# Batch 3's keys and queries loaded in three parts, with the first part re-laid out ahead of batch 2's last FFN units

## The chip, the cores and the metric

The kernel runs on one core of a Trainium2 chip. The metric is the device time of one execution in microseconds, as a median of several runs: 398.33 us for the kernel before (three runs, 398.25 to 398.63). A profiled execution is longer than its own span by what lies before the first and behind the last instruction.

Names of engines below: PE is TensorE (matmul), PEld its weight loads, DVE is VectorE, ACT is ScalarE, POOL is GpSimd, SP is SyncE. POOL and SP work here as issuers of DMAs more than as engines; an issued DMA is carried out by 16 DMA engines that the issuers' queues share.

## The reference

Sigmoid attention over 8 batches, 12 heads, 448 positions and a head size of 64, followed by a gated feed-forward network (FFN) over the 3584 rows that the attention gives:

```python
scores = scale * np.matmul(q, k.transpose(0, 1, 3, 2)) - np.log(S)
attn = 1.0 / (1.0 + np.exp(-scores))
x = np.matmul(attn, v)            # heads put side by side: 3584 x 768
gate = np.maximum(x @ w_gate, 0.0)
val = x @ w_val
out = gate * val @ w_out          # 1536 -> 768
```

## The kernel before

**Attention.** The heads of a batch are worked in three groups `g` of four heads. For QK, keys and queries have to stand with the head's 64 elements on the partitions. They come from DRAM the other way round, converted to fp16 on the way (`load`, line 106, issued on POOL's queue). For batch 2 and later they are turned by `dma_transposes(b, g)` (line 211): two DVE copies re-lay a group's keys and queries into a tile `rel` (line 215, 128 x 896 each), and one DMA transpose, issued on SP's queue, turns `rel` into `qkT` (line 219). `rel` has two buffers, `qkT` three. A QK unit (`qk_unit`, line 292) takes one of seven column blocks of a group: 4 matmuls on PE into two PSUM banks, and two sigmoids on ACT. The 21 units of a batch go group by group, seven units each; after a group's seventh unit its product with V (`pv_group`, 28 matmuls) follows a few units later.

**FFN.** Batches 0 and 1 are multiplied with `w_gate` and `w_val` in units `gv` (line 304): 12 matmuls, a ReLU on ACT, a product on DVE into `hT` (line 327). Later batches, and the product with `w_out`, go in pairs with fewer block products (`gv_pair`, `down_pair`), which need sums of blocks made ahead on DVE: `weight_sums(i)` (line 376, 1.35 us each) makes the four sums of `w_out`'s blocks.

**The order.** The schedule is manual: each engine's queue has the order in which the code calls. Batch `b`'s loop (line 692) cuts the 21 QK units into stretches `m` by `cuts`, and behind each stretch come FFN units. For batch 2, `mix` says how many `gv` units follow each stretch, and `hooks[m]` puts other work between them: a hook `(left, work)` runs when `left` units are still to come. `ffn_mix` (line 574) does that:

```python
for left in range(count, -1, -1):
    while hooks and hooks[0][0] >= left:
        hooks.pop(0)[1]()
    if left:
        gv_queue.popleft()()
```

Batch 2's last stretch (`m` = 5) has three QK units, two `gv` units and a `down_pair` (line 758), whose `jobs` run behind its first product. In the kernel before, the hooks of this stretch are `weight_sums(1)` between the two units and `weight_sums(2)` behind them, and the jobs are `dma_transposes(3, 0)` and `dma_transposes(3, 1)` followed by `weight_sums(3)`. `dma_transposes(3, 2)` comes in batch 3's first stretch.

**Loads.** Batch 3's keys, queries and values are loaded in batch 2's first stretch (line 750): one load each for `k` and `q`, and three for `v` (`load_v`). On POOL's queue they stand behind batch 2's values and the two loads of `w_out` (`load_o`), and ahead of `hold(3, 2)` (line 645), a small copy on POOL that waits until a transpose has landed, and batch 4's loads. The tiles `k16` and `q16` have one buffer from batch 2 on, so a load waits until the batch before it has been re-laid out.

Of the kernel before, what the change touches and what calls it, by code (L numbers as in the profile page):

```python
# [17 lines left out]
def kernel(  # L18
# [75 lines left out]
    def tiles_of(b):  # L94
        if b not in in_tiles:
            pool = early if b == 1 else inp
            in_tiles[b] = tuple(
                p.tile([P, NPAIR, NCH * D], FP16, tag=t, name=t)
                for p, t in ((pool, "k16"), (pool, "q16"), (vinp, "v16"))
            )  # L100
        return in_tiles[b]

    def rows_of(src, b):
        return src[b].rearrange("(x r) (t c) d -> (r t) x (c d)", r=2, c=NCH)

    def load(b, g0, g1, which, c0=0, c1=NCH):
        for nm, t16, src in zip("kq", tiles_of(b), (k, q)):
            if nm in which:
                xs, cs = slice(2 * g0, 2 * g1), slice(c0 * D, c1 * D)
                nc.gpsimd.dma_start(t16[:, xs, cs], rows_of(src, b)[:, xs, cs])  # L110

    def load_v(b):
        v16 = tiles_of(b)[2]
        nc.gpsimd.dma_start(v16[:, 0::2, :], rows_of(v, b)[:, 0::2, :])
        for r in range(2):
            nc.gpsimd.dma_start(
                v16[64 - 64 * r : P - 64 * r, 1::2, :], rows_of(v, b)[64 * r : 64 * r + 64, 1::2, :]
            )
# [71 lines left out]
    def qkT_of(b, g):  # L190
        if (b, g) not in qkT_tiles:
            qkT_tiles[(b, g)] = qkTp.tile([P, TW, P], FP16, tag="qkT", name="qkT")
        return qkT_tiles[(b, g)]
# [17 lines left out]
    def dma_transposes(b, g):  # L211
        k16, q16, _ = in_tiles[b]
        rel = relp.tile([P, TW, P], FP16, tag="rel", name="rel")
        for ti, t16 in enumerate((k16, q16)):
            nc.vector.tensor_copy(  # L215
                rel[:, ti * NCH : (ti + 1) * NCH, :].rearrange("p c (h d) -> p h c d", h=2),
                t16[:, 2 * g : 2 * g + 2, :].rearrange("p h (c d) -> p h c d", c=NCH),
            )
        nc.sync.dma_start_transpose(
            qkT_of(b, g)[:], rel[:].rearrange("p c x -> p (c x)")  # L220
        )
# [70 lines left out]
    def qk_unit(b, g, c):  # L292
        ps = [bank("qk_ps") for _ in range(2)]
        qk(qkT_tiles[(b, g)], c, 0, NCH, lambda hh: ps[hh][:, 0:S])
        PT = PTp.tile([P, 2, S], FP16, tag="PT", name="PT")
        for hh in range(2):
            sigmoid(PT[:, hh, 0:S], ps[hh][:, 0:S])
        PT_tiles[(b, g, c)] = PT

    def pv_group(b, g):  # L300
        pv(b, g, 0, S, [PT_tiles.pop((b, g, c))[:, :, 0:S] for c in range(NCH)])
# [66 lines left out]
    def open_late():  # L368
        first_sbuf.close()
        pool = ctx.enter_context(tc.tile_pool(name="late", bufs=1))  # L370
        late["T"] = pool.tile([P, 4, HF, HM], FP16, tag="T", name="T")
        late["X"] = pool.tile([P, 3, HD, S], FP16, tag="X", name="X")
        late["sums"] = ctx.enter_context(tc.tile_pool(name="sums", bufs=2))

    def sub(o, a, b):
        nc.vector.tensor_tensor(out=o, in0=a, in1=b, op=AOP.subtract)
# [18 lines left out]
    def weight_sums(i):  # L395
        T = [late["T"][:, j] for j in range(4)]
        B11, B21 = wo[:, 0:HF, 0:HM], wo[:, HF:NFC, 0:HM]
        B12, B22 = wo[:, 0:HF, HM:DM], wo[:, HF:NFC, HM:DM]
        sub(T[i], *((B12, B11), (B22, T[0]), (B22, B12), (B21, T[1]))[i])
# [96 lines left out]
    def batch_sums_t1(g):  # L496
        T1, _, _, B11, _, B12, _ = batch_blocks(g, (0, HD))
        sub(T1, B12, B11)

    def batch_sums(g, ks):  # L500
        T1, T2, T4, _, B21, B12, B22 = batch_blocks(g, ks)
        sub(B12, B22, B12)
        sub(T2, B22, T1)
        sub(T4, B21, T2)
# [69 lines left out]
    def ffn_mix(count, hooks=()):  # L574
        hooks = list(hooks)
# [5 lines that stand above are left out]
# [56 lines left out]
    def pv_finish(b):  # L637
        pv_group(b, NG - 1)
        if b < 2:
            push_gv(b, 0, S, range(NFC))  # L640
# [4 lines left out]
    def hold(b, g):  # L645
        nc.gpsimd.tensor_copy(gate[0:1, :], qkT_tiles[(b, g)][0:1, 0, 0:2])

    def both(b, g):
        pe_transposes(b, g, 0)
        pe_transposes(b, g, 1)  # L650
# [10 lines left out]
    def push_group(g):  # L661
        tail = [("t", g, 6)] + [("y", g, p) for p in range(3)]
        if g == 0:
            tail.insert(0, tail.pop(1))
        work.extend([("w", g, f) for f in range(0, NFC, 2) if g > 0] + tail)
# [26 lines left out]
    for b in range(1, B):  # L692
        if b == 1:
            cuts, pv_at = (0, 3, 6, 9, 13, 17, 21), {3: (0, 2), 5: (1, 2)}
        elif b == 2:
            cuts, pv_at = (0, 4, 7, 11, 14, 18, 21), {0: (-1, 2), 2: (0, 2), 4: (1, 2)}
        else:
            cuts, pv_at = (0, 4, 8, 12, 16, 21), {0: (-1, 2), 2: (0, 2), 4: (1, 2)}
        count = len(cuts) - 1
        hooks = {}  # L700
        if b == 1:
            mix = (3, 3, 3, 3, 3, 2)
            hooks = {
                1: [(1, lambda: both(1, 1))],
                3: [(1, lambda: both(1, 2))],
                4: [(3, lambda: dma_transposes(2, 0))],
                5: [(2, late_loads)],
            }
        elif b == 2:
            mix = (2, 2, 1, 1, 1, 2)  # L710
            hooks = {
                2: [(0, prepare)],
                4: [(0, lambda: weight_sums(0))],
                5: [(1, lambda: weight_sums(1)), (0, lambda: weight_sums(2))],
            }
            open_late()
        elif b == 3:
            mix = (1, 1, 1, 0, 0)
        else:
            mix = (0,) * count  # L720
        for m in range(count):
            jobs = []
            for i, (g, c) in enumerate(order[cuts[m] : cuts[m + 1]]):
                if m in pv_at and i == pv_at[m][1]:
                    if m == 0:
                        pv_finish(b - 1)
                        if b == 2:
                            push_group(0)
                        elif b % 2 == 0:
                            push_group(b // 2 - 1)  # L730
                    else:
                        pv_group(b, pv_at[m][0])
                qk_unit(b, g, c)
            if m == 0 and b > 1:
                jobs.append(lambda: dma_transposes(b, 2))
            if b == 2 and m == count - 1:
                jobs.append(lambda: (dma_transposes(3, 0), dma_transposes(3, 1)))
            elif b == 3 and m == count - 1:
                jobs.append(lambda: (dma_transposes(4, 0), dma_transposes(4, 1)))
            elif 0 <= m - count + 2 and 3 < b < B - 1:  # L740
                jobs.append(lambda: dma_transposes(b + 1, m - count + 2))
            if b == 1:
                if m == 0:
                    load(2, 0, 1, "kq")
                    load(2, 1, 2, "kq")
                    load(2, 2, 3, "kq")
            elif m == 0 and b + 1 < B:
                if b == 3:
                    jobs.append(lambda: hold(3, 2))
                jobs.append(lambda: (load(b + 1, 0, 3, "kq"), load_v(b + 1)))  # L750
            if b % 2 and b > 2:
                if m == count - 1:
                    jobs.append(lambda: (batch_sums_t1(b // 2), batch_sums(b // 2, (0, 1))))
            elif b > 3 and m == 0:
                jobs.append(lambda: batch_sums(b // 2 - 1, (1, HD)))
            if b == 2 and m == count - 1:
                ffn_mix(mix[m], hooks[m])
                next_work(jobs + [lambda: weight_sums(3)], first_act=True)
            elif mix[m]:
                for job in jobs:  # L760
                    job()
                ffn_mix(mix[m], hooks.get(m, ()))
            else:
                next_work(jobs)
            if b == 3 and m in (1, 3):
                for f in range(*((0, 8, 2), (8, NFC, 2))[m // 2]):
                    gate_sums(f, f + 2)
# [35 lines left out]
```

## Time and profile before

| what | us |
|---|---|
| median of 3 runs | 398.33 |
| the profiled execution | 399.14 |
| its span | 397.3 |
| PE busy | 388.5 |
| DVE, ACT, POOL busy | 279.6, 223.2, 49.5 |
| batch 2's last two gv units on PE | 89.37 to 94.1 |
| its down_pair on PE | 93.9 to 100.9 |
| batch 3's first QK units on PE | from 101.36 |
| batch 3's loads of k, q: issue, time to landing | 74.0, 18.4 and 74.8, 21.0 |
| w_out's second load: issue, time to landing | 73.0, 16.0 |
| transpose of batch 3's group 0: issue, time to landing | 96.75, 4.6 |

Times within the profile count from the first instruction. The busy time of PE is 98% of the span, but the end of a matmul is modelled, so an idle stretch of PE is what tells of a wait. A line of the timeline or of a group gives the engine, the line of the code, the operation, what it writes `<-` what it reads, shapes, and in brackets how long the engine had been idle and what ended that. "SPq" and "POOLq" are the issuing queues of these engines. In the DMA view q0 is the queue of POOL's loads, q1 that of the transposes and stores issued by SP and ACT, and q8 and q14 fetch instructions; its columns are packets, MB and the time that the packets took as a share of 16 engines' time (over 100% where packets overlap).

### The profile page before, as it was taken

What the parts mean: (1) busy time and instruction counts of PE and PEld (TensorE: products, weight loads), DVE (VectorE), ACT (ScalarE), POOL (GpSimd) and SP (SyncE); (2) the same over time, 40 slices, a digit from 0 to 9 for tenths busy, and PEclk for the clock granted to TensorE, in tenths of its full rate; (3) what the DMA queues carried; (4) which work ended last, traced back from release to release, by engine and by line L of the source; (5) the groups of instructions that cost most, each with busy time, mean ns of one, the idle gap of its engine ahead of it and who ended that gap; (6) DMA issues with size and microseconds to landing.
All of it is one profiled execution on the core that took longest, in us unless ns stands there. A gap on an engine that the chain in (4) does not pass through costs nothing.

```text
span 397.3 us, 8744 instructions
## 1 busy us (share of the span) xinstructions
PE 388.5 (98%) x3488; PEld 217.5 (55%) x3488; DVE 279.6 (70%) x539; ACT 223.2 (56%) x476; POOL 49.5 (12%) x73
## 2 busy tenths in 40 slices
PE   8999999999999999999999999999999999999995
PEld 3678686445455554554555555455455555555563
DVE  3453345358377889999758889999776779987662
ACT  5946768684785565655665455565566233543121
POOL 8643400700030300003000300000000000000000
PEclk9999999999999999999999999999999999999999
DMA  9999994999999893224945695222013320000135
GB/s 150 196 198 204 206 129 87 180 203 190 203 143 180 167 218 53 46 48 54 177 84 133 130 219 89 48 21 57 19 40 81 81 79 2 0 1 2 40 94 146
DMA packets 68953, 43.69 MB, mean 110 GB/s; under 512 B 35888, under 2 KB 65584, under 8 KB 68912
## 3 DMA queue, kind: packets, MB, share of 16 engines
q0 software_dynamic: 30736, 23.33, 39.2%
q1 hardware_dynamic: 37744, 19.34, 23.2%
q8 instruction: 27, 0.44, 0.4%
q10 hardware_dynamic: 432, 0.46, 0.4%
q14 instruction: 14, 0.11, 0.1%
HBM read 47.19 MB, written 11.01 MB: 146 GB/s over the span
## 4 chain that ended last, share of the span: by engine, by line
PE 84%; DMA 11%; POOL 2%; ACT 1%; issue 0%; DVE 0%; ACTq 0%; POOLq 0%; DVEq 0%
PE u L385 32%; PE g L385 15%; PE y L385 8%; PE qk_ps L232 7%; PE pv_ps L250 7%; PE g_ps L309 5%; PE v_ps L309 5%; DMA wg<-in_moe_w_gate_dram 4%; DMA v<-in_v_dram 3%; PE ya L346 3%; DMA q<-in_q_dram 2%; PE yb L346 1%; DMA qkT<-rel 1%; ACT PT L187 1%; POOL k L110 1%; POOL q L110 1%
## 5 line engine op out<-in xcount | busy, mean ns | idle before, releaser
L187 ACT ACTIVATE PT<-qk_ps 128x448 f16<-128x448 f32 (+3 forms) x318 | 150.5, 595 | 72.6 <-PE qk_ps L232 72.5
L385 PEld LDWEIGHTS <-S 128*128 128x128 f16 x540 | 52.8, 98 | 43.6
L536 DVE TENSOR_TENSOR gsb<-g,gsb 128x448 f32<-128x448 f32 x72 | 42.9, 625 | 14.6 <-PE g L385 14.1
L232 PE MATMUL qk_ps<-qkT 64*64 64x448 f16 (+2 forms) x756 | 49.9, 336 | 1.3 <-DVE qkT L206 0.5
L421 ACT ACTIVATE ysb<-u 128x384 f32<-128x384 f32 x27 | 13.4, 498 | 53.4 <-PE u L385 53.4
L327 DVE TENSOR_TENSOR hT<-gate_sb,v_ps 128x256 f16<-128x256 f32 (+2 forms) x36 | 16.2, 465 | 34.7 <-ACT gate_sb L318 22.3
L532 ACT COPY gsb<-u 128x448 f32<-128x448 f32 x48 | 25.7, 566 | 23.9 <-PE u L385 22.9
L250 PE MATMUL pv_ps<-PT,v 64*64 64x448 f16 (+2 forms) x756 | 37.7, 329 | 1.1 <-DMA v<-in_v_dram 0.8
L184 DVE TENSOR_SCALAR xT<-pv_ps 128x448 f16<-128x448 f32 (+2 forms) x53 | 27.9, 567 | 15.2 <-PE pv_ps L250 13.8
L385 PEld LDWEIGHTS <-hT 128*128 128x128 f16 x288 | 27.7, 98 | 19.8 <-issue 2.1
L232 PEld LDWEIGHTS <-qkT 64*64 64x64 f16 x756 | 20.0, 105 | 25.5 <-issue 16.3
L309 PE MATMUL v_ps<-xT,wv 128*128 128x256 f16 (+2 forms) x216 | 33.3, 290 | 0.3 <-DMA wv<-in_moe_w_val_dram 0.3
L309 PE MATMUL g_ps<-xT,wg 128*128 128x256 f16 (+2 forms) x216 | 33.5, 291 | 0.1
L385 PEld LDWEIGHTS <-wv 128*128 128x128 f16 x216 | 21.1, 98 | 19.7
L385 PEld LDWEIGHTS <-wg 128*128 128x128 f16 x216 | 20.3, 98 | 20.6 <-issue 3.0
L250 PEld LDWEIGHTS <-v 64*64 64x64 f16 x756 | 21.8, 107 | 12.8 <-DMA v<-in_v_dram 1.5
L385 PE MATMUL u<-T,hT 128*128 128x384 f16 x144 | 27.3, 326 | 0.0
L437 DVE SCALAR_TENSOR_TENSOR ysb<-y,ysb 128x384 f32<-128x384 f32 x24 | 13.4, 557 | 17.8 <-PE y L385 10.3
L309 PEld LDWEIGHTS <-wg 128*128 128x128 f16 x216 | 18.5, 98 | 11.5 <-issue 5.0
L110 POOL DMA_DIRECT2D k<-in_k_dram x14 | 10.9, 780 | 110.7 <-DVE rel L215 104.4
L309 PEld LDWEIGHTS <-wv 128*128 128x128 f16 x216 | 20.1, 98 | 7.9 <-DMA wv<-in_moe_w_val_dram 0.6
L385 PE MATMUL u<-xT,wg 128*128 128x448 f16 x108 | 23.5, 353 | 0.1
(69 smaller groups left out, 531.0 us busy)
## 6 DMA issues: line engine op xcount, KB each, us to landing
out_dram<-ysb SPq DMA_DIRECT2D x52, 192.0 KB, 3.0
k<-in_k_dram POOLq DMA_DIRECT2D x5, 672.0 KB, 11.7
q<-in_q_dram POOLq DMA_DIRECT2D x5, 672.0 KB, 14.9
v<-in_v_dram POOLq DMA_DIRECT2D x8, 336.0 KB, 15.4
v<-in_v_dram POOLq DMA_DIRECT2D x16, 168.0 KB, 15.2
k<-in_k_dram POOLq DMA_DIRECT2D x8, 224.0 KB, 10.4
wo<-in_moe_w_out_dram POOLq DMA_DIRECT2D x1, 1536.0 KB, 13.1
q<-in_q_dram POOLq DMA_DIRECT2D x6, 224.0 KB, 11.3
```

What stands on the lines that cost most here:

```text
L110: nc.gpsimd.dma_start(t16[:, xs, cs], rows_of(src, b)[:, xs, cs])
L184: nc.vector.tensor_scalar(out=xT, in0=src, scalar1=XSCALE, scalar2=None, op0=AOP.mult)
L187: nc.scalar.activation(PT_ap, ps_ap, AF.Sigmoid, bias=sig_bias, scale=qk_scale)
L232: nc.tensor.matmul(out_of(hh)[o : o + 64, :], qkT[rows, c, cols], qkT[rows, NCH + c0 : NCH + c1, cols], start=True, stop=True, tile_positi ...
L250: nc.tensor.matmul(ps[hh][64 * r : 64 * r + 64, 0:qn], v16[rows, 2 * g + hh, c * D : (c + 1) * D], pieces[c][rows, hh, :], start=(c == 0), ...
L309: nc.tensor.matmul(ps[-1][:, 0:qn], wt[:, dc, f * P : (f + 1) * P], xT_tiles[b][:, dc, q0 : q0 + qn], start=(dc == 0), stop=(dc == NDC - 1),)
L327: nc.vector.tensor_tensor(out=hT_tiles[g][:, f, o : o + qn], in0=gate_sb[:, 0:qn], in1=ps[1][:, 0:qn], op=AOP.mult,)
L346: nc.tensor.matmul(ps[:, 0 : m1 - m0], hT_tiles[g][:, f, t * P : (t + 1) * P], wo[:, f, m0:m1], start=(f == 0), stop=(f == NFC - 1),)
L385: nc.tensor.matmul(ps[:, 0:n], A[:, k_, :], W[:, k_, :], start=(first and k_ == 0), stop=(k_ == kn - 1), skip_group_check=True,)
L421: nc.scalar.activation(o, ps[:, 0:HM], AF.Copy, scale=OUT_SCALE)
L532: by(gs[u][i][:], ps[u][:, 0:S])
L536: nc.vector.tensor_tensor(out=gs[u][i][:], in0=ps[u][:, 0:S], in1=gs[u][i][:], op=AOP.add)
```

## The change

Batch 3's keys and queries are loaded group by group, six loads instead of two, in the order k and q of group 0, of group 1, of group 2; the bytes are the same. `dma_transposes(3, 0)`, that is two DVE copies and the DMA transpose, is moved from the jobs of batch 2's last `down_pair` to a hook ahead of the two last `gv` units. `dma_transposes(3, 1)` stays where it is. Other batches' loads and transposes are not changed.

```diff
                 4: [(0, lambda: weight_sums(0))],
-                5: [(1, lambda: weight_sums(1)), (0, lambda: weight_sums(2))],
+                5: [
+                    (2, lambda: dma_transposes(3, 0)),
+                    (1, lambda: weight_sums(1)),
+                    (0, lambda: weight_sums(2)),
+                ],
...
             if b == 2 and m == count - 1:
-                jobs.append(lambda: (dma_transposes(3, 0), dma_transposes(3, 1)))
+                jobs.append(lambda: dma_transposes(3, 1))
...
-                jobs.append(lambda: (load(b + 1, 0, 3, "kq"), load_v(b + 1)))
+                def load_next():
+                    for g0, g1 in ((0, 1), (1, 2), (2, 3)) if b == 2 else ((0, 3),):
+                        load(b + 1, g0, g1, "kq")
+                    load_v(b + 1)
+
+                jobs.append(load_next)
```

## The prediction

> **What bounds the kernel now.** I read the page first: TensorE (PE) is busy for 388.5 of 397.3 us, so only an idle stretch of PE can be won or made. The busy table by windows says where those are.
>
> ```profile
> 100.90:101.40 0.50, 0.06 (x5) 0.05 (x8) 0.00 (x0) 0.45 (x1) 0.00 (x0) 1.00 1.28 224
> 101.40:393.00 291.60, 291.12 (x2218) 155.12 (x2218) 232.48 (x438) 153.74 (x334) 14.84 (x21) 1.00 0.46 87
> ```
>
> The columns are stretch, length, then busy us (and instructions) of PE, weight loads, DVE, ACT, POOL, then clock, DMA share, GB/s. From 101.4 us on PE lacks 0.48 us in 291.6, so whatever delays it at 101.4 is paid at the end nearly in full, and whatever is won there is kept. The chain of waits from 85 to 105 us shows what ends the idle stretch.
>
> ```profile
> 96.03 0.72 PE u L385 x5
> 96.75 4.56 DMA qkT<-rel
> 101.31 0.04 issue
> 101.36 0.57 PE qk_ps L232 x8
> ```
>
> Batch 3's first QK units wait for the transpose of its group 0, which was issued at 96.75 us and landed at 101.31. PE's work before that ends at 100.91 (the list of waits puts 0.4 us on it, the idle time before 101.36 in the timeline is 0.45). So the place that the change touches holds **0.45 us, 0.11% of the time**: no gain can be larger, and it is under the 0.2% that a measurement of this kernel can tell from no change (0.80 us). A loss has no such ceiling.
>
> The timeline shows DVE around the new place of the re-layout.
>
> ```profile
> 89.39 1.35 DVE L376 TENSOR_TENSOR T<-wo 128x2304 f16<-128x2304 f16 x1
> 92.36 0.62 DVE L327 TENSOR_TENSOR hT<-gate_sb,v_ps 128x448 f16<-128x448 f32 x1 [1.62 <-ACT gate_sb L318]
> 96.75 4.87 SPq L219 DMA_TRANSPOSE qkT<-rel  x2
> ```
>
> Last, the DMA view. Loads (q0) and transposes (q1) share the 16 DMA engines. Three windows: loads alone (89 to 92 us), both together (138 to 141), a transpose alone (106 to 108.5).
>
> ```profile
> q0 software_dynamic: 701, 0.61, 126.4%
> ...
> q0 software_dynamic: 514, 0.45, 91.1%
> q1 hardware_dynamic: 516, 0.13, 33.2%
> ...
> q1 hardware_dynamic: 1789, 0.46, 98.5%
> ```
>
> The first number is packets. Loads alone pass 701 in 3 us, 234 a us. A transpose alone passes its 1,789 packets in 2.3 us (the DMA row of that window is empty until 106.25), 780 a us. Together they take turns one for one, 514 to 516 in 3 us: **a transpose beside loads runs at 172 packets a us, under a quarter of its pace**.
>
> **The change part by part.**
>
> *Three loads for each of k and q.* POOL issues six loads instead of two. An issue of a third takes 0.71 us (batch 2's, at 40 to 49 us), of a whole 0.84: 6 x 0.71 - 2 x 0.84 = 2.6 us more on POOL, which idles from 77.6 to its hold at 109.3 waiting for a transpose. So this costs nothing itself. Behind these on POOL's queue stand V's three loads. In the built program POOL's loads take eight completion semaphores in turn, and with four loads more V's parts come onto those of the two wo loads and of k's first third, and wait for them. By the DMA issues wo's second part was issued at 73.0 and landed 16.0 later, at 89.0; the first landed at 85.1. So V is issued at about 85, 89 and 90 us, still ahead of its turn (q lands at 74.8 + 21.0 = 95.8), and the load queue doesn't run dry. PE needs V only at batch 3's first PV group, at 110 us. Nothing on the path. Packets per byte stay the same.
>
> *When the first third is there.* After wo (89.0), k landed at 74.0 + 18.4 = 92.4 and q at 95.8, so 3.4 us for each, 1.13 for a third: k's group 0 at 90.1, q's at 91.3.
>
> *The re-layout moved.* Two DVE copies of 0.39 us go from behind weight sum 2 (96.0 us) to behind weight sum 0, which ends at 89.39 + 1.35 = 90.74. The k copy runs at once, the q copy waits until 91.3 and ends at 91.7. DVE had nothing to do until 92.36, so it costs nothing there; the cover is 0.66 us. If q's third came later than 92.0, the hT product at 92.36 behind it, and the banks that it frees, would be late. At its old place it takes 0.6 us away before weight sum 3, which PE's last product needs only at 99.8: no gain.
>
> *The transpose moved.* SP issues it when the copies are done (0.07 us later at the old place), at 91.8 instead of 96.75. SP has nothing between: group 1's transpose and the stores from 101.7 on keep their order behind it. Its first packets come 1.15 us after the issue (105.11 to 106.25), at 92.95. This is what the change is about, and here it meets the loads, as the DMA view of 92.9 to 99 us shows:
>
> ```profile
> q0 software_dynamic: 1178, 1.00, 102.4%
> q1 hardware_dynamic: 487, 0.12, 20.8%
> q8 instruction: 1, 0.02, 0.9%
> q14 instruction: 1, 0.01, 0.3%
> ```
>
> 1,178 load packets are still to come. Taking turns, they and 1,178 of the transpose's 1,790 need 1,178 / 172 = 6.85 us, to 99.8. The other 612 at 780 a us need 0.8, to 100.6. From last packet to landing 109.2 - 108.5 = 0.7 us: **101.3 us, to a tenth the landing of before**. Five microseconds of earlier issue are given to the loads: before, the transpose came to engines that had just run out of them.
>
> *The instruction fetch.* The last two lines above are fetches, at 93 and 96 us. Where a fetch falls into a transpose beside loads, all engines stand still for a while. The transpose issued at 183.9 had one; this is the GB/s row of 184 to 195 us, 0.275 us a figure:
>
> ```profile
> GB/s 0 0 0 2 95 153 164 163 145 142 140 116 133 146 154 170 168 162 175 172 170 181 191 192 197 202 191 187 194 242 182 187 183 101 50 25 9 121 191 207
> ```
>
> The fall to 101, 50, 25, 9 is about 1.2 us. The three transposes issued together with loads landed 10.6 us (225.3, no fetch), 11.5 (183.9, a fetch) and 12.2 us after issue (133.8, a fetch): 0.9 and 1.6 more. Before, the fetch at 96 us fell ahead of the transpose's packets, though a shorter hole of some 0.75 us shows at 98.5. Now it falls in the middle. I add 1.1 us: landing at 102.4. The ends: without a hole 101.3 (and 0.4 less if the count is generous, 100.9); with the full 12.2 us of the worst row, 91.8 + 12.2 = 104.0. I stand near 91.8 + 10.6 = 102.4, the row without a fetch but with more loads beside it than here; two ways to the same figure.
>
> *What follows.* PE's wait is then 102.4 + 0.05 - 100.9 = 1.55 us instead of 0.45, **+1.1 us**. Group 1's transpose queues behind it: 102 + 2.3 + 0.7 = 105.0, needed by batch 3's eighth unit at about 107 + 1.1. V, pushed back by some 3.5 us from 99.4, is needed at 110 + 1.1. The hold and batch 4's loads shift with PE. Sum: 399.14 (profiled execution: span 397.3 and 1.84 around it) + 1.1 = 400.2; that execution stands 0.81 above the median, so the prediction is 398.33 + 1.1 = **399.4 us**.
>
> *A rule weighed.* The row first: the load queue's 126.4% share from 89 to 92 us says that the engines have no spare time where the transpose now goes. The Trainium skill (Perfetto Trace Analysis, DMA Optimizations) says that splitting DMAs can let some of the work start sooner, and expects a sooner end if the DMA engines are generally idle. Taken without its condition it gives a landing at 91.8 + 4.1 = 95.9, PE's wait gone and 398.7 us for the profiled execution; by the rows it is 400.2, since the condition doesn't hold here.
>
> **The rivals.**
>
> *Likeliest, 0.60: late by a hole or by more sharing*, landing 102.0 to 103.4, 399.0 to 400.4 us.
>
> *A draw, 0.22*: landing 101.0 to 101.7, between -0.3 and +0.4 us, 398.0 to 398.7. For it: the count of packets without a fetch. Against: a fetch falls in the window, and fetches cost both transposes that had one beside loads.
>
> *It does what it says, 0.10*: the transpose lands before 100.9, PE doesn't wait, 398.33 - 0.45 = 397.9. This is the other side. The place is the same wait of PE at 101.36; it decides if the transpose needs no more than 9.1 us from its issue at 91.8. For it: 4.1 us with free engines, and the loads end before it does. Against: 10.6 to 12.2 us in all three cases with loads.
>
> *Worse, 0.08*: 12.2 us, or a first third that lands after 92 us and holds DVE, landing at 104 or later: +2.7, 401.0.
>
> **How the numbers follow.** 80%: 398.1 leaves out most of the third case, 400.7 most of the last and the edge of the first. The likeliest's own range is 399.0 to 400.4. Slower by over 0.2% (399.13): most of the likeliest and the last, 0.62. Faster by over 0.2% (397.53) needs 0.8 us where 0.45 are to be had: 0.03 for what I haven't seen. The rest, 0.35, within.
>
> **What the profile after would show.** Right: the transpose issued at about 91.8 and landing at 102 or later; PE idle for over 1 us before batch 3's first qk_ps, ended by that DMA; q0 and q1 with equal packet counts from 94 to 99 us; V landing at about 103 instead of 99.4; DVE's hT still at 92.4. Wrong: the transpose landing in under 9 us although the loads run (no taking turns), or rel's q copy far from 91.5 (thirds land otherwise), or a wait elsewhere, such as V in batch 3's first PV group.

## The result, and the profile after

The changed kernel takes 399.16 us (median of 11 runs, 398.90 to 400.33) against 398.33 of the kernel before: a ratio of 1.0022 with a 95% interval of 1.0014 to 1.0030, 0.83 us slower. The prediction was 399.4.

Where it is lost, two views of the changed kernel's profile show. The chain of waits from 85 to 110 us (start, length, what):

```profile
90.09 0.96 PE v_ps L309 x6
91.06 10.47 DMA qkT<-rel
101.52 0.04 issue
101.57 0.57 PE qk_ps L232 x8
```

The transpose of batch 3's group 0 is issued 5.7 us earlier than before (91.06 against 96.75) and lands 0.2 us later (101.52 against 101.31): it takes 10.47 us where it took 4.56. Lines of the timeline around it:

```profile
90.60 0.39 DVE L215 COPY rel<-q 128x896 f16<-128x896 f16 x1
91.06 10.06 SPq L219 DMA_TRANSPOSE qkT<-rel  x2
91.77 0.62 DVE L327 TENSOR_TENSOR hT<-gate_sb,v_ps 128x448 f16<-128x448 f32 x1 [0.78 <-ACT gate_sb L318]
101.57 0.57 PE L232 MATMUL qk_ps<-qkT 64*64 64x448 f16 x8 [1.25 <-DMA qkT<-rel]
```

PE's idle time ahead of batch 3 has grown from 0.45 to 1.25 us. These 0.80 us agree with the 0.83 us of the medians. Behind it nothing has changed, as the busy table by windows says (PE had 291.12 busy of these 291.60 us before):

```profile
101.40:393.00 291.60, 291.09 (x2218) 155.15 (x2218) 232.53 (x438) 153.74 (x333) 14.88 (x21) 1.00 0.46 87
```

The spans of the two profiles (397.3 and 397.5 us) differ by only 0.2: in the profile after, PE's work ahead of the wait ends at 101.57 - 1.25 = 100.32 us, 0.59 earlier than before. That comes from ahead of the change: a transpose at 63 us is already 0.75 earlier (issued at 62.97 against 63.72), and the first load that the change touches is issued at 73 us. In the profile before PE waited 0.78 us for V's load at 48 us, in that after it did not. Times within profiles are therefore to be read against the end of PE's work in the same profile.

### The profile page after: what moved, and what is told of

Same layout as the page of the kernel before. It is cut to its first block, busy times and chain, and to the rows that moved or that the text cites. A ratio compares the mean times of both kernels' runs of the same rounds, so it can differ in the third digit from the quotient of the medians.

```text
span 397.5 us, 8750 instructions
## 1 busy us (share of the span) xinstructions
PE 388.7 (98%) x3488; PEld 218.0 (55%) x3488; DVE 279.9 (70%) x539; ACT 223.3 (56%) x476; POOL 52.2 (13%) x77
## 4 chain that ended last, share of the span: by engine, by line
PE 93%; ACT 3%; DMA 3%; DVE 1%; issue 0%; ACTq 0%; DVEq 0%
PE u L385 32%; PE g L385 15%; PE qk_ps L232 9%; PE y L385 8%; PE pv_ps L250 8%; PE g_ps L309 7%; PE v_ps L309 7%; PE ya L346 3%; DMA qkT<-rel 3%; ACT PT L187 2%; PE warm_ps L175 1%; PE yb L346 1%; PE trt L201 1%; DVE qkT L206 0%; ACT ysb L421 0%
## 5 line engine op out<-in xcount | busy, mean ns | idle before, releaser
L110 POOL DMA_DIRECT2D k<-in_k_dram x16 | 12.3, 768 | 111.1 <-DVE rel L215 104.5
```

## The experiments

The theory, A: what the moved transpose gains by its early issue it loses again to the loads that run beside it, and a fetch that falls into it adds to that. The rivals: the split loads or the late V cost the time (C); the issue on SP is what is slow (B); DVE's new order costs it. The table has all runs of the study, with the landing of group 0's transpose and PE's idle time ahead of batch 3 (from each kernel's profile), and the ratio of times to the kernel before on the same chip. The kernel before ran again beside each set of runs; its median was 398.42 us beside split alone, move alone and the two kernels with all of V behind, and 398.33 beside the rest. The diffs are cut to the lines that matter and are against the changed kernel, except for "before, V behind" and "before, fetch moved", which are against the kernel before.

| kernel | issue, us to landing | PE idle ahead of batch 3 | median us | ratio, 95% interval |
|---|---|---|---|---|
| before | 96.75, 4.6 | 0.45 | 398.33 | 1 |
| changed | 91.06, 10.5 | 1.25 | 399.16 | 1.0022 (1.0014 to 1.0030) |
| split alone | 96.53, 4.7 | 0.58 | 398.26 | 0.9998 (0.9989 to 1.0006) |
| move alone | 94.97, 4.9 | 0, but 2.4 ahead of it | 400.73 | 1.0059 (1.0043 to 1.0074) |
| changed, V behind | 91.17, 7.3 | 0 | 398.25 | 0.9992 (0.9983 to 1.0001) |
| changed, half of V behind | 90.78, 9.0 | 0 | 398.07 | 0.9993 (0.9983 to 1.0002) |
| before, V behind | 95.60, 4.1 | 0, but 1.4 later | 399.85 | 1.0032 (1.0021 to 1.0042) |
| changed, one unit later | 92.57, 7.6 | 0.34 | 398.11 | 0.9992 (0.9983 to 1.0001) |
| changed, fetch moved | 91.56, 9.7 | 0.82 | 399.00 | 1.0014 (1.0005 to 1.0023) |
| before, fetch moved | 96.41, 4.3 | 0.16 | 398.61 | 1.0006 (0.9997 to 1.0015) |

### The split alone

```diff
-                    (2, lambda: dma_transposes(3, 0)),
...
-                jobs.append(lambda: dma_transposes(3, 1))
+                jobs.append(lambda: (dma_transposes(3, 0), dma_transposes(3, 1)))
```

> The loads in three parts alone, the transpose of group 0 at its old place. If the loss comes from the moved transpose (theory A), six loads instead of two and the later issue of V cost nothing: the time of before, 398.3 us to 0.3 us, PE's wait ahead of batch 3 0.45 us as before. If the split itself costs (rival: the later V, or thirds that move fewer bytes a microsecond), most of the 0.8 us is here: 398.9 to 399.2 us.

398.26 us, a ratio of 0.9998. PE's wait is close to that of before, in this kernel's timeline:

```profile
101.27 0.38 PE L232 MATMUL qk_ps<-qkT 64*64 64x448 f16 x4 [0.58 <-DMA qkT<-rel]
```

The six loads and the later issue of V cost nothing that can be measured. C falls.

### The move alone

```diff
-                    for g0, g1 in ((0, 1), (1, 2), (2, 3)) if b == 2 else ((0, 3),):
+                    for g0, g1 in ((0, 3),):
```

> The re-layout and transpose moved, with whole loads. Group 0's q copy then waits for the whole of q (95.8 us in the profile before), DVE stands from 90.7 to there, and weight sums 1 to 3 behind it come late: sum 1 ends at 95.8 + 0.4 + 0.6 + 1.35 = 98.2 instead of 94.25, and PE's second product with it, at 95.9 before, waits 2.3 to 2.7 us. Both theories: about 2.3 us above before, 400.6 us (400.0 to 401.3), with the idle time of PE inside the down_pair and the transpose no longer what PE waits for. If the old place was harmless for DVE, it stays at 399.2.

400.73 us, where 400.6 was expected. The list of waits from 88 to 104 us (engine and line, what it waited for, us in total, times, longest):

```profile
DVE rel L215 <- DMA q<-in_q_dram: 3.0, 1, 3.0
PE u L385 <- DVE T L376: 1.9, 1, 1.9
```

DVE waits for the whole of q, and PE for the weight sum queued behind it. So the split is what makes the new place possible at all. PE's wait for the transpose is gone here, and it helps nothing: a later one has taken its place.

### V behind the transpose

```diff
-                    (2, lambda: dma_transposes(3, 0)),
+                    (2, lambda: (dma_transposes(3, 0), hold(3, 0), load_v(3))),
...
-                    load_v(b + 1)
+                    if b != 2:
+                        load_v(b + 1)
```

> The changed kernel, but batch 3's V is loaded only after the transpose of group 0 has landed (a second small POOL copy that waits for it). Theory A (the transpose is late because loads share the DMA engines with it): the loads beside it end with q, at about 95 us; 520 packets taking turns at 172 a us from 92.2 are through at 95.2, the other 1,270 at 780 a us at 96.9, landing at 97.6, with a hole of 1.2 us 98.8. PE no longer waits: 398.33 - 0.45 = 397.9 us. Theory B (what is slow is the issue on SP, 3.9 us to the first packet in the changed kernel, whatever is queued): first packet at 95, landing at 97.8, 397.9 us too; the time to the first packet tells them apart (1.2 us by A, 3.9 by B). If V's load has no part in it, 399.2 us.

The transpose lands at 98.45, and PE goes from the `down_pair` into batch 3's QK units without a gap; the chain of waits has no DMA in it:

```profile
99.39 0.97 PE u L385 x6
100.36 0.50 PE qk_ps L232 x8
```

398.25 us: 0.91 below the changed kernel, and 0.9992 of before, where 0.9989 was expected; the interval reaches to 1.0001, so that it beats the kernel before isn't shown. That V's load, which in this stretch does nothing but run beside the transpose, is what made the changed kernel slower than before is shown. The first packet came 2.4 us after the issue, neither A's 1.2 nor B's 3.9. The source view of the transpose's line, for the changed kernel and then for this one (how long SP took to issue it, in ns; then the landing):

```profile
L219 SPq DMA_TRANSPOSE qkT<-rel x1: 4616/4616/4616, 91.1 to 91.1; - x1
DMA to landing us min/median/max: 10.5/10.5/10.5
```

```profile
L219 SPq DMA_TRANSPOSE qkT<-rel x1: 2268/2268/2268, 91.2 to 91.2; - x1
DMA to landing us min/median/max: 7.3/7.3/7.3
```

B and A are both right in part: the issue itself gets longer, and with the loads. DVE's order is that of the changed kernel here, so it isn't what costs the time either.

### Half of V behind it

`load_v` is given the parts to load; the first of its three stays in front, the two others follow `hold(3, 0)`.

```diff
-                    (2, lambda: dma_transposes(3, 0)),
+                    (2, lambda: (dma_transposes(3, 0), hold(3, 0), load_v(3, ((0, 1),)))),
...
-                    load_v(b + 1)
+                    load_v(b + 1, (0, ()) if b == 2 else (0, (0, 1)))
```

> Between the changed kernel and the one with V behind the transpose: the first of V's three loads (half of its bytes) stays in front, the two others wait until the transpose has landed. The transpose landed 10.5 us after its issue with all of V beside it and 7.3 with none. If it is the loads beside it that cost, about the middle: 8.9 us, landing at 100.0 in the changed kernel's profile, just before PE needs it; no wait or up to 0.3 us of it, 398.0 to 398.4 us. If only the last of the loads in the queue matter, 10.5 us and 399.2.

9.0 us from issue to landing, between 7.3 and 10.5 as expected, and an issue between the two (line numbers are one higher in this kernel):

```profile
L220 SPq DMA_TRANSPOSE qkT<-rel x1: 3207/3207/3207, 90.8 to 90.8; - x1
DMA to landing us min/median/max: 9.0/9.0/9.0
```

It lands at 99.80, just as PE is through with its work; no wait is left, 398.07 us. That this is faster than the kernel before isn't shown (the interval reaches to 1.0002). With none, half and all of V beside it the transpose takes 7.3, 9.0 and 10.5 us. Each of the three has a fetch among its packets, so that the difference between them is in the main the loads'.

### V behind, at the old place

```diff
-                jobs.append(lambda: (dma_transposes(3, 0), dma_transposes(3, 1)))
+                jobs.append(
+                    lambda: (dma_transposes(3, 0), dma_transposes(3, 1), hold(3, 0), load_v(3))
+                )
...
-                jobs.append(lambda: (load(b + 1, 0, 3, "kq"), load_v(b + 1)))
+                jobs.append(lambda: (load(b + 1, 0, 3, "kq"), b == 2 or load_v(b + 1)))
```

> The kernel before, and nothing changed but V's load, which waits until group 0's transpose has landed. If the 0.45 us that PE waits before is itself due to loads beside the transpose, it lands 4.0 us after its issue at 96.75, at 100.7, before PE needs it: 397.9 us. If the hole in the DMA traffic at 98.5 us comes from the instruction fetch at 96 and not from the loads' end, it lands at 101.3 as before: 398.3 us. If V now comes too late for batch 3's first PV group (at 110 us), over 398.8.

With the loads out of the way the transpose takes 4.1 us and lands before PE needs it, as expected. But V, issued at 100.3 us among the stores, comes too late. Source view of the transpose, then the list of waits from 95 to 131 us:

```profile
L219 SPq DMA_TRANSPOSE qkT<-rel x1: 1508/1508/1508, 95.6 to 95.6; - x1
DMA to landing us min/median/max: 4.1/4.1/4.1
```

```profile
PE pv_ps L250 <- DMA v<-in_v_dram: 1.2, 1, 1.2
PE qk_ps L232 <- DMA qkT<-rel: 0.2, 1, 0.2
```

399.85 us, 1.4 above before (398.42). The profile shows 1.0 of this: 0.45 won, 1.2 lost at the first PV group and 0.2 at batch 4's first QK units. It is that of an execution of 399.42 us, 0.4 below the median, so where the rest goes isn't shown. The wait of 0.45 us could be had without any split; but V can't wait that long.

### The transpose one FFN unit later

```diff
-                    (2, lambda: dma_transposes(3, 0)),
-                    (1, lambda: weight_sums(1)),
+                    (1, lambda: (dma_transposes(3, 0), weight_sums(1))),
```

> The changed kernel with the re-layout and transpose behind the first of the two gv units instead of ahead of both, so issued at about 93.2 us instead of 91.1 (in the profile of the changed kernel), still into the loads. If sharing with the loads sets the landing, an earlier or later issue hardly matters, since all packets have to be through anyway: landing 101.0 to 101.6, 398.9 to 399.2 us as the changed kernel. If it is the 10.5 us from issue to landing that are fixed (sharing packet by packet to the end), landing at 103.7 and 401.3 us. In both the first packet should come as the loads run out, 2 to 4 us after the issue, if a running load stream holds up the issue itself; 1.2 us after it if not.

A miss in time: 398.11 us. The transpose is issued 1.5 us later than in the changed kernel and lands 1.4 us earlier, at 100.13. The expectation of the first packet was right: none from 93 to 96 us, then 3.9 us after the issue (96.5 us), as the loads thinned out (their last packet came at 98.3). What was not expected was that it would land earlier. The changed kernel's transpose has packets from 94.9 on, and a fetch at 95.9 falls into them; here the fetch comes at 95.25, ahead of the first packet. The GB/s row of the DMA view, first the changed kernel from 91 to 102 us (0.275 us a figure), then this one from 92 to 101 (0.225 us a figure):

```profile
GB/s 205 196 202 199 225 216 202 205 209 196 199 202 205 205 196 198 199 247 181 180 185 148 50 24 8 118 199 177 217 225 165 150 96 130 287 277 291 173 293 287
```

```profile
GB/s 224 187 207 211 203 195 195 215 211 203 199 211 199 207 256 191 191 183 203 205 184 221 233 143 103 87 90 89 162 288 289 291 275 290 233 205 288 291 290 289
```

The hole down to 8 GB/s at 97 to 98 us is missing in the second row. A slower stretch (96 there, 87 to 103 here) stands in both where the last loads drain. The missing hole is not all of the gain: PE's wait is 0.91 us shorter than in the changed kernel, and the next run, which takes only the fetch away, wins 0.43. The rest comes with the later issue; why, no run here shows.

### The fetch moved

```diff
-    keep_warm(10)
+    keep_warm(2)
+    few_ps = bank("warm_ps")
+    for _ in range(36):
+        nc.tensor.matmul(few_ps[:, 0:64], zeros[:, 0:P], zeros[:, 0:64], start=True, stop=True)
+    free.rotate(1)
```

> The changed kernel with 56 more instructions at the start of PE's stream (8 of the 10 warming matmuls of 448 columns replaced by 36 of 64 columns), so that the instruction fetch that fell at 95.9 us, into the transpose, falls some 5 us earlier, ahead of its first packet; the work is the same. If the hole of 1.2 us in the DMA traffic behind the fetch is part of what the change costs, the transpose lands 1.2 us earlier, at 100.3, PE's wait of 1.25 us goes to about 0.1 and the time is 398.0 us, against 399.2; less if another hole takes its place. If the hole has nothing to do with the fetch, it stays at 96.8 to 98.0 us and the time at 399.2. The start itself may differ by some tenths of a microsecond.

The fetch moved to 92.8 us, by 3 us where 5 were expected, and the deep hole is gone. The DMA view from 91 to 102 us, and the timeline:

```profile
GB/s 205 199 205 205 205 196 295 179 179 176 182 196 205 202 205 196 206 196 193 192 113 149 164 164 185 169 190 124 143 98 120 93 128 284 279 288 171 289 290 290
```

```profile
101.33 0.38 PE L232 MATMUL qk_ps<-qkT 64*64 64x448 f16 x4 [0.82 <-DMA qkT<-rel]
```

But only 0.74 us of the 10.47 are won, not 1.2, since the stretch of 93 to 143 GB/s, where the last loads drain, is longer here. PE's wait is 0.82 instead of 1.25 us. The same edit in the kernel before is the control:

> The same 56 instructions added to the kernel before: the control of the run above. Before, the fetch at 96.3 us fell just ahead of the transpose's packets and a hole of 0.75 us stood at 98.5. If that hole comes from the fetch, the landing moves from 101.3 to 100.6, PE's wait of 0.45 goes, 397.9 us; if it comes from the loads' end, the time stays at 398.4 us but for the start.

```profile
100.73 0.38 PE L232 MATMUL qk_ps<-qkT 64*64 64x448 f16 x4 [0.16 <-DMA qkT<-rel]
```

There the wait goes from 0.45 to 0.16 us, and yet the time is 398.61, not lower than before: the new warming leaves PE idle for 0.75 us at 4.75 us, ahead of its first transposes. (The loads in flight at the issue also landed sooner here, 2.0 us after it instead of 2.7, so the 0.29 are not the fetch's alone.) Against this control the changed kernel with the fetch moved is 0.39 us slower, where the pair without the edit differs by 0.83. The intervals are too wide (0.0009 either way) to call the difference of these differences measured in time. In the profiles, one for each kernel, the change costs 0.80 us of PE's wait without the edit (0.45 to 1.25) and 0.66 with it (0.16 to 0.82). So the fetch is the smaller part of the loss at most; the larger stays with V's load, which the runs with V behind took away although a fetch still fell into their transposes.

## Why the prediction was right, and where its steps were not

*The place holds 0.45 us, what is lost there is lost at the end*: right. 0.80 us more of PE's wait, 0.83 us more time.

*The split costs nothing, V waits for wo's semaphores*: right, by the run with the split alone. V's issue on POOL's queue in the changed kernel's timeline, expected at 85, 89 and 90 us:

```profile
84.85 0.76 POOL L114 DMA_DIRECT2D v<-in_v_dram  x1 [7.29 <-DMA wo<-in_moe_w_out_dram]
88.54 0.64 POOL L116 DMA_DIRECT2D v<-in_v_dram  x1 [2.92 <-DMA wo<-in_moe_w_out_dram]
89.67 0.63 POOL L116 DMA_DIRECT2D v<-in_v_dram  x1 [0.49 <-DMA k<-in_k_dram]
```

V landed at 100.4 us, which is 101.0 on the clock of the profile before: 1.6 later than the 99.4 there, not 3.5.

*The copies fit into DVE's idle time*: right. The q copy ran at 90.60, and hT came at 91.77, which is the 92.36 of before less the 0.59 by which that profile runs ahead.

*The first packets come 1.15 us after the issue*: wrong. This is the step that failed. The 1.15 were read off a transpose with no loads beside it. Here SP needed 4.6 us for the issue and the first packet came after 3.9. From 92.3 to 94.8 us the DMA view of the changed kernel has loads and a fetch, and no transpose:

```profile
q0 software_dynamic: 594, 0.50, 125.4%
q14 instruction: 1, 0.01, 0.8%
```

*1,178 load packets and as many of the transpose take turns, 6.85 us*: the turns were right, their number wasn't. From 95 to 96.8 us:

```profile
q0 software_dynamic: 313, 0.26, 88.7%
q1 hardware_dynamic: 293, 0.08, 30.6%
```

313 to 293 in 1.8 us, 174 and 163 a us, against 172 expected. But the transpose joined 2.7 us later than I had it, so it ran beside the loads for only some 5 us, a hole among them, with few loads left from 99 on and none from 100.1. Its last packets then ran at 287 GB/s, some 1,120 of 256 B a us, where I had 780.

*A hole of 1.1 us by the fetch*: right in place and size (97 to 98 us). The run with the fetch moved shows that the deep hole is the fetch's; what stays where the loads drain is not. Of the 1.6 us that I read off the transpose at 133.8 us, though, only some 0.9 are the fetch's: without one it takes 11.3 to 11.4 us there (the two runs with the fetch moved), not 10.6.

*The landing*: 102.4 expected, 10.6 us after the issue; measured 10.47. The wrong start hardly entered the sum, since the loads run at their full pace while the transpose is held up. An estimate with the prediction's prices (234 load packets a us alone, 172 in turns, 780 for the transpose alone, 1.1 for the hole, 0.7 to the landing) and the 1,224 load packets that this profile has from 92.2 us on: a first packet at 92.2 lands the transpose at 101.9, one at 94.9 at 101.7; measured 101.5. That the nearest row, 10.6, held as well is luck in part: that transpose was issued just ahead of the loads' packets, its issue took 1.6 us and its first packet came after 1.2. The size of the whole, +1.1 against +0.83, is off because the transpose's lead over PE's end was 9.26 us (100.32 - 91.06) where I counted 9.1, and the landing 0.1 us faster.

*The rivals.* By its landing alone, 101.52, the result looks like the draw (101.0 to 101.7). But that profile runs ahead: 101.52 with PE's work done at 100.32 corresponds to 102.1 on the clock of the profile before, at the lower edge of the likeliest's 102.0 to 103.4. That the change does what it says was to happen below 9.1 us from issue to landing: the runs with 9.0, 7.6 and 7.3 us have PE waits of 0, 0.34 (issued 1.5 us later) and 0. Its place and its price were right; loads beside the transpose kept it from happening.

## What to carry to other kernels

An earlier issue is an earlier landing only if the DMA engines have room: see in the DMA view how many packets of other queues are still to come, and take the duration from a transfer that ran in such company, not from one that ran alone. If a transfer on the critical path must start early, look at what stands in the same stretch and isn't urgent, here V; moving half of that behind it took PE's wait away, which the early issue alone could not (a time below that of before isn't shown). And before moving work to win a wait, read how long the wait is: 0.45 us here, less than the move put at risk.

## What the runs showed of the hardware

**A running load stream holds up the issue of a transpose.** I had expected sharing of the engines, not a longer issue. Among transposes issued into loads that already run, the longer these still run, the longer SP takes (from the profiles of this study; the first packet is that of the transpose, us after its issue):

| kernel | last load lands after the issue, us | SP's issue, us | first packet, us | transpose, us to landing |
|---|---|---|---|---|
| before, V behind | none in flight | 1.5 | 1.2 | 4.1 |
| before, fetch moved | 2.0 | 1.7 | 1.2 | 4.3 |
| before | 2.7 | 2.1 | 1.2 | 4.6 |
| split alone | 2.9 | 2.3 | 1.2 | 4.7 |
| move alone | 3.1 | 2.3 | 1.6 | 4.9 |
| changed, V behind | 4.0 | 2.3 | 2.4 | 7.3 |
| changed, one unit later | 6.0 | 3.1 | 3.9 | 7.6 |
| changed, half of V behind | 6.1 | 3.2 | 3.8 | 9.0 |
| changed, fetch moved | 8.6 | 4.8 | 3.9 | 9.7 |
| changed | 9.4 | 4.6 | 3.9 | 10.5 |

What goes with a long issue is load packets that move during it, not loads that are still to come. The transposes at 133.8, 183.9 and 225.3 us in the profile before were issued together with loads that landed 9.7 to 11.7 us later, but at most one load packet fell into their issue: it took 1.6 to 1.7 us, the first packet came after 1.2, and yet they took 10.6 to 12.2 us.

In most rows of the table an instruction fetch falls into the issue or up to 0.6 us ahead of it, and a fetch can lengthen an issue too: a transpose at 63 us with no loads beside it was issued in 1.5 us in the changed kernel and in 2.6 with the fetch moved, where a fetch came 0.5 us behind the start of the issue. A transpose further on has no fetch near its issue: that of batch 3's group 2, at 103.5 to 105.3 us. With no load running it was issued in 1.5 us in the changed kernel. Where V, put behind, was still loading beside it, it took 3.9 us (before, V behind), 3.3 (changed, V behind) and 2.6 (half of V behind). So running loads lengthen an issue with no fetch near; how much of each row above is theirs isn't shown.

Stores on SP's own queue don't do that: the transpose at 105.1 us in the profile before was issued behind stores that kept the engines busy to 106, and took 1.55 us. By what means the loads hold up the issue no run here tells.

**A fetch into a transpose stops all DMA engines for about 1 us.** It did in the changed kernel (8 GB/s at the lowest); with half of V behind, where the fetch at 96.5 fell into the transpose, the row of 91 to 100 us has a longer one:

```profile
GB/s 187 203 215 199 240 179 203 203 207 211 183 211 199 215 203 207 189 199 202 257 227 101 59 75 141 98 267 234 17 0 3 9 9 9 133 289 276 289 291 291
```

It did not where the fetch came ahead of the transpose's packets (one unit later, fetch moved). The place of the fetch depends on the number of PE's instructions: 56 more at the start moved it by 3 us. They moved later fetches too, which gives a control that the edit was not made for. The transpose at 183.9 us, beside loads, took 11.2 to 11.6 us in the eight kernels where a fetch fell into it and 10.65 and 10.70 in the two with the fetch moved, where none did; at 225 us it is the other way round, 10.4 to 10.9 without and 11.8 and 11.6 with one. At 216 us, with no loads beside it, the transpose took 5.6 to 5.7 us with a fetch in six kernels, 4.2 with one in two, and 3.95 without in the two with the fetch moved.

**Where loads drain beside a transpose, the traffic falls to some 60 to 150 GB/s for about 1 us**, with and without a fetch near (in the rows above 87 to 103 one unit later, 93 to 143 with the fetch moved, 59 to 141 with half of V behind). The transpose with no load in flight (before, V behind) has no such fall: a mean of 215 GB/s from 96.9 to 98.6 us. The cause stays open.
